# Values cast once for a pair of chunks, weights loaded earlier, and w_out in runs of four rows, in a fused recurrence and squared-ReLU kernel

## The chip, the cores and the metric

The kernel runs on one core of a Trainium2 chip. The metric is the device time of one execution in microseconds (us); lower is better. Each comparison ran the changed kernel and the kernel before on the same chip in the same rounds. Every ratio in this text is the mean time of one kernel's fast runs over that of the other's of the same rounds, with a 95% interval, so it is not quite the ratio of the medians that stand beside it. "Faster" and "slower" as verdicts mean by more than 2%.

Engines: PE is TensorE's matmuls, PEld its weight loads, DVE is VectorE, ACT ScalarE, POOL GpSimd, SP SyncE.

## The reference

A gated linear recurrence over 768 steps for 4 x 8 heads of width 48, then a two-layer FFN with the square of a ReLU:

```
f = 1 / (1 + exp(-f_logit))
state = f[t] * state + outer(k[t], v[t]);  y[t] = q[t] @ state      # 768 steps, 32 heads
x = y as (3072, 384);  h = max(x @ w_in, 0);  out = (h * h) @ w_out # w_in (384, 2048), w_out (2048, 384)
```

Inputs and output are fp32; the matmuls run in bf16.

## The kernel before

The recurrence is computed in 24 chunks of 128 steps, taken in 12 pairs ("attention"). Two chunks make one FFN group of 256 columns: `mm1` multiplies by w_in into `hp` (576 matmuls), ACT or DVE apply ReLU and square, `mm2` multiplies by w_out into `op` (384 matmuls). A small planner inside the kernel simulates all steps with estimated durations and fixes the order of each engine's instructions when the kernel is built. On the chip each engine then keeps to that order. The names in the lines below: `pc` are the running sums of log f of a pair, `tr` transposes of q and k, `at` the products of k and q within a chunk, `am` these times a mask, `ds` a pair's contribution to the state, `sz` the state, `yp` a chunk's y, `xp` and `xT` its transpose; `vx` and `vz` are the values in bf16, in `vz` some of them moved to the other 64 partitions; `idle` is filler that no result needs. `LEAD` shifts the rank of attention against the FFN in the plan. The planner also has a model of the DMA queues: each transfer has an estimated time (`data=`), and GpSimd's queue gets 0.7 of the engines when both queues are busy.

The parts that matter here (cuts marked `...`):

```python
    LEAD = 8
    PACE = [7, 10, 14, 16, 16, 18, 18, 18]        # after which input each weight slice is issued
    ...
    w_in = const.tile([C, KS, d_ff], BF16)         # one tile, 128 x (3 x 2048)
    w_out = const.tile([C, FS, d_model], BF16)
    wo_view = moe_w_out.rearrange("(fs p) f -> p fs f", p=C)
    ...
            if kind == "i":
                nc.gpsimd.dma_start(w_in[:, :, s * FW:(s + 1) * FW], wi_view[:, :, s * FW:(s + 1) * FW])
            else:
                nc.gpsimd.dma_start(w_out[:, s * FQ:(s + 1) * FQ, :], wo_view[:, s * FQ:(s + 1) * FQ, :])
        ...
        plan.add(f"cw{kind}{s}", "POOL", 0.8, fn, after=after, rank=-1, data=(2.8, 0))
    ...
        def vx():                                  # the half that has to change partitions
            st["vx", n] = work.tile([C, H, D], BF16, tag="vx", bufs=3, name="vx")
            for z, j, vt in halves(n):
                nc.gpsimd.tensor_copy(st["vx", n][z], vt[z, 1 - j])
        ...
        def vs():                                  # DMA moves it: vz <- vx
            ...
        def vc():                                  # the half that stays
            for z, j, vt in halves(n):
                nc.gpsimd.tensor_copy(new_vz()[z, j], vt[z, j])
    ...
                        nc.tensor.matmul(ds[j][:, pr, :], a[z, NP + pr, r],
                                         (vt[z, j] if r == j else vo[z])[:, 2 * pr:2 * pr + 2, :].rearrange("p h d -> p (h d)"), ...)
    ...
                        nc.tensor.matmul(hp[:, x, :], w_in[:, ks, (f + x) * C:(f + x + 1) * C], xT[:, ks, lo:lo + W], ...)
```

## Time and profile before

| kernel before | |
|---|---|
| time, median of 3 | 193.49 us (192.4 to 193.5) |
| span of the profiled run | 190.7 us |
| PE / PEld / DVE / ACT / POOL busy | 92 / 70 / 65 / 66 / 49% |
| first hp matmul, first op matmul | 24.0 us, 51.6 us |
| slices of w_in issued | 13.6, 22.2, 32.9, 40.5 us |
| slices of w_out issued | 41.2 to 43.9 us |

The share of TensorE is an average over two regimes. Up to some 60 us the core loads inputs at a full DMA and TensorE often has nothing useful to do; from there to 181 us it is full. So a change earns time only by getting useful matmuls done early. The prediction below shows the lines.

### The profile page before, as it was taken

To read this page: it belongs to the slowest core of one execution; us is meant where nothing else is said; L and a number is where in the kernel's file an instruction comes from. 1 tells how busy PE (TensorE), PEld (TensorE's weight loads), DVE (VectorE), ACT (ScalarE), POOL (GpSimd) and SP (SyncE) were. 2 spreads that over 40 slices of the span, in tenths; PEclk is the share of its full clock that TensorE was granted. 3 is DMA by queue.
4 is the path that set the end of the run, shared out by engine and by line. 5 is a ranking of instruction groups with operands and counts; after the bars stand their busy time and mean duration, and the time that the engine had idled before them with its cause. 6 is when DMAs were issued, how large, how long until landed. Compare 5 with 4: busy or idle time off the path is not lost.

```text
span 190.7 us, 4962 instructions
## 1 busy us (share of the span) xinstructions
PE 176.0 (92%) x1953; PEld 132.8 (70%) x1953; DVE 124.9 (65%) x240; ACT 125.5 (66%) x239; POOL 93.2 (49%) x194
## 2 busy tenths in 40 slices
PE   7578789898999999999999999999999999999991
PEld 7466577786787766667677777677786777777760
DVE  7568897989978847726977646975666735433200
ACT  3646578879879887143896577588485765755521
POOL 7588539595902393926973484652663224000000
PEclk9969999999999999999999999999999999999998
DMA  6999999999998079999999989999561374121122
GB/s 156 261 263 238 270 211 272 243 273 207 204 207 206 3 135 295 209 284 207 218 279 132 262 159 293 186 244 231 98 138 21 65 136 80 22 62 46 41 56 68
DMA packets 77719, 33.29 MB, mean 175 GB/s; under 512 B 71808, under 2 KB 76736, under 8 KB 77696
## 3 DMA queue, kind: packets, MB, share of 16 engines
q1 hardware_dynamic: 71488, 25.11, 65.9%
q0 software_dynamic: 6208, 7.87, 20.2%
q8 instruction: 15, 0.25, 0.6%
q14 instruction: 8, 0.07, 0.1%
HBM read 25.17 MB, written 4.72 MB: 157 GB/s over the span
## 4 chain that ended last, share of the span: by engine, by line
PE 72%; DVE 10%; ACT 6%; POOL 5%; DMA 3%; issue 2%; POOLq 0%; ACTq 0%
PE op L640 32%; PE hp L595 27%; DVE az L423 4%; DMA w_in<-in_moe_w_in_dram 3%; PE at L515 3%; PE yp L541 3%; PE pc L389 2%; ACT ep L412 2%; POOL mask L326 2%; PE ds L479 2%; DVE am L525 1%; DVE le L400 1%; ACT en L412 1%; POOL sz L502 1%; PE pc L392 1%
## 5 line engine op out<-in xcount | busy, mean ns | idle before, releaser
L595 PE MATMUL hp<-xT,w_in 128*128 128x256 bf16 x576 | 75.3, 273 | 4.1 <-ACT hr L602 1.6
L640 PE MATMUL op<-w_out,hT 128*128 128x384 bf16 x384 | 72.9, 326 | 0.0
L595 PEld LDWEIGHTS <-w_in 128*128 128x128 bf16 x576 | 54.6, 98 | 17.1 <-issue 4.5
L602 ACT ACTIVATE hr<-hp 128x512 bf16<-128x512 f32 x82 | 48.4, 596 | 24.7 <-PE hp L595 23.2
L611 DVE TENSOR_TENSOR hT<-hr 128x512 bf16<-128x512 bf16 x69 | 30.3, 443 | 33.8 <-ACT hr L602 33.3
L640 PEld LDWEIGHTS <-hT 128*128 128x128 bf16 x384 | 35.9, 98 | 18.5
L502 POOL TENSOR_TENSOR sz<-tm,en 48x192 bf16<-48x192 f32 x40 | 21.6, 540 | 32.2 <-DVE tm L493 18.8
L525 DVE TENSOR_TENSOR am<-at,mask 128x512 bf16<-128x512 f32 x48 | 31.5, 681 | 4.3 <-PE at L515 4.3
L656 POOL DMA_DIRECT2D out_dram<-ob x36 | 19.2, 537 | 29.0 <-ACT ob L650 29.0
L650 ACT COPY ob<-op 128x384 f32<-128x384 f32 x22 | 10.5, 476 | 16.6 <-PE op L640 16.0
L609 ACT ACTIVATE hT<-hr 128x512 bf16<-128x512 bf16 x27 | 16.9, 631 | 1.0 <-DVE hr L604 0.3
L363 POOL CAST vx<-io_v 64x384 bf16<-64x384 f32 x24 | 13.9, 578 | 4.0 <-DMA io_v<-in_v_dram 2.8
L423 DVE TENSOR_TENSOR az<-io_q,en 128x384 bf16<-128x384 f32 x24 | 14.8, 619 | 0.4 <-ACT en L412 0.3
L423 DVE TENSOR_TENSOR az<-io_k,ep 128x384 bf16<-128x384 f32 x24 | 14.3, 594 | 0.8 <-ACT ep L412 0.8
L381 POOL CAST vz<-io_v 64x384 bf16<-64x384 f32 x24 | 13.6, 569 | 1.1
L674 PE MATMUL idle<-zero 128*128 128x128 bf16 x139 | 12.2, 252 | 1.0 <-DVE zero L312 1.0
L375 POOL DMA_DIRECT2D vz<-vx x24 | 13.1, 549 | 0.0
L350 ACT ACTIVATE e<-io_f 128x768 f32<-128x768 f32 x12 | 10.2, 848 | 3.6 <-DMA io_f<-in_f_logit_dram 3.5
L549 ACT CAST ys<-yp 128x384 bf16<-128x384 f32 x18 | 8.5, 482 | 5.0 <-PE yp L541 5.0
L352 ACT ACTIVATE pz<-e 128x384 bf16<-128x384 f32 x24 | 11.2, 515 | 0.4
L674 PEld LDWEIGHTS <-zero 128*128 128x128 bf16 x139 | 10.6, 117 | 1.0 <-DVE zero L312 1.0
L400 DVE TENSOR_TENSOR le<-pc,pz 128x384 f32<-128x384 f32 x12 | 6.7, 555 | 6.6 <-ACT ep L412 6.1
(54 smaller groups left out, 173.4 us busy)
## 6 DMA issues: line engine op xcount, KB each, us to landing
io_f<-in_f_logit_dram SPq DMA_DIRECT2D x12, 384.0 KB, 5.7
io_k<-in_k_dram SPq DMA_DIRECT2D x12, 384.0 KB, 6.5
io_q<-in_q_dram SPq DMA_DIRECT2D x12, 384.0 KB, 6.4
io_v<-in_v_dram SPq DMA_DIRECT2D x12, 384.0 KB, 6.2
out_dram<-ob POOLq DMA_DIRECT2D x36, 96.0 KB, 3.9
w_in<-in_moe_w_in_dram POOLq DMA_DIRECT2D x4, 384.0 KB, 7.4
w_out<-in_moe_w_out_dram POOLq DMA_DIRECT2D x4, 384.0 KB, 12.6
vz<-vx POOLq DMA_DIRECT2D x24, 48.0 KB, 4.7
```

The source lines that it names most:

```text
L363: nc.gpsimd.tensor_copy(st["vx", n][z], vt[z, 1 - j])
L381: nc.gpsimd.tensor_copy(new_vz()[z, j], vt[z, j])
L423: nc.vector.tensor_mul(z.rearrange("p y (x d) -> p y x d", x=2)[:, :, :, :D], st[x, n].rearrange("p (y x) r d -> p y x r d", x=2)[:, :, :, ...
L502: nc.gpsimd.tensor_mul(nx[r, :, D * x:D * (x + 1)], tm[r, :, D * x:D * (x + 1)], g.unsqueeze(2).to_broadcast([D, NP, D]))
L525: nc.vector.tensor_mul(t, st["at", i][x], mask.rearrange("p y s t -> p y (s t)"))
L595: nc.tensor.matmul(hp[:, x, :], w_in[:, ks, (f + x) * C:(f + x + 1) * C], xT[:, ks, lo:lo + W], start=(ks == 0), stop=(ks == KS - 1), skip ...
L602: nc.scalar.activation(hr[:, :m, :], st["hp", c0, f][:, :m, :], AFT.Relu)
L609: nc.scalar.activation(st["hT", g][:, f:f + m, lo:lo + W], hr[:, :m, :], AFT.Square)
L611: nc.vector.tensor_mul(st["hT", g][:, f:f + m, lo:lo + W], hr[:, :m, :], hr[:, :m, :])
L640: nc.tensor.matmul(st["o", i], hT[:, fs, tt * C:(tt + 1) * C], w_out[:, fs, :], start=(fs == 0), stop=(fs == FS - 1))
L656: (nc.gpsimd if soft else nc.sync).dma_start(out[row + r:row + C:2, :], st["ob", i][P2 * r:P2 * (r + 1)])
L674: nc.tensor.matmul(idle, zero, zero)
```

## The change

Its intent: cast the values of both chunks once (12 larger casts on GpSimd or ACT instead of 48 small ones on GpSimd), move one half by DMA and copy the other on any free engine; issue the weights earlier (PACE, LEAD); read w_out so that each partition gets four consecutive rows in one run of 6 KB. The last needs the hidden units in a matching order, so the weight loads of w_in now take every fourth column.

```diff
-    LEAD = 8
-    PACE = [7, 10, 14, 16, 16, 18, 18, 18]
+    LEAD = 6
+    PACE = [7, 7, 7, 8, 8, 13, 14, 14]
...
-    wo_view = moe_w_out.rearrange("(fs p) f -> p fs f", p=C)
+    wo_view = moe_w_out.rearrange("(s p x) f -> p s x f", p=C, x=FQ)
...
-        plan.add(f"cw{kind}{s}", "POOL", 0.8, fn, after=after, rank=-1, data=(2.8, 0))
+        plan.add(f"cw{kind}{s}", "POOL", 0.8, fn, after=after, rank=-1, data=(2.6 if kind == "i" else 2.3, 0))
...
+        def vx(e):
+            t = st["vx", n] = work.tile([C, 2, H, D], BF16, tag="vx", bufs=3, name="vx")
+            copy[e](t, st["v", n].rearrange("p h r d -> p r h d"))
+        plan.add(f"vx.{n}", "POOL", 1.1, lambda: vx("POOL"), also=[("ACT", 0.75, lambda: vx("ACT"))], ...)
...
+        def vc(e):
+            for j in range(2):
+                z = slice(P2 * j, P2 * (j + 1))
+                copy[e](new_vz()[z, j], st["vx", n][z, j])
...
-                                         (vt[z, j] if r == j else vo[z])[:, 2 * pr:2 * pr + 2, :]...
+                                         vt[z, r, 2 * pr:2 * pr + 2, :]...            # vt is vx now, ds needs no vz
...
-                        nc.tensor.matmul(hp[:, x, :], w_in[:, ks, (f + x) * C:(f + x + 1) * C], xT[:, ks, lo:lo + W],
+                        nc.tensor.matmul(hp[:, x, :], units(ks, f + x), xT[:, ks, lo:lo + W],
...
+    def units(ks, f):
+        s, x = divmod(f, FQ)
+        return w_in[:, ks, s * FW:(s + 1) * FW].rearrange("k (p x) -> k x p", x=FQ)[:, x]
```

More of the change, by code (lines that the diff above doesn't have):

```diff
@@ L261 @@
     st = {}
-    copy = {"ACT": nc.scalar.copy, "DVE": nc.vector.tensor_copy}
+    copy = {"ACT": nc.scalar.copy, "DVE": nc.vector.tensor_copy, "POOL": nc.gpsimd.tensor_copy}
     def both(name, dve, act, fn, **kw):
@@ L299, in fn @@
             else:
-                nc.gpsimd.dma_start(w_out[:, s * FQ:(s + 1) * FQ, :], wo_view[:, s * FQ:(s + 1) * FQ, :])
+                nc.gpsimd.dma_start(w_out[:, s * FQ:(s + 1) * FQ, :], wo_view[:, s])
         after = [] if not pace else [f"vx.{c}"] if x == "v" else [f"{x}{c}"]
-        plan.add(f"cw{kind}{s}", "POOL", 0.8, fn, after=after, rank=-1, data=(2.8, 0))
+        plan.add(f"cw{kind}{s}", "POOL", 0.8, fn, after=after, rank=-1, data=(2.6 if kind == "i" else 2.3, 0))
     touch = const.tile([C, 1], F32)
@@ L353, in attention @@
         plan.add(f"a1.{n}", "ACT", 1.7, a1, after=[f"f{n}"], take=["pz"], give=[f"io_f:f{n}"])
-        def halves(n):
-            vt = st["v", n].rearrange("p h r d -> p r h d")
-            return [(slice(0, P2), 0, vt), (slice(P2, C), 1, vt)]
-        def vx():
-            st["vx", n] = work.tile([C, H, D], BF16, tag="vx", bufs=3, name="vx")
-            for z, j, vt in halves(n):
-                nc.gpsimd.tensor_copy(st["vx", n][z], vt[z, 1 - j])
-        plan.add(f"vx.{n}", "POOL", 0.95, vx, after=[f"v{n}"], take=["vx"], rank=-2)
+        def vx(e):
+            t = st["vx", n] = work.tile([C, 2, H, D], BF16, tag="vx", bufs=3, name="vx")
+            copy[e](t, st["v", n].rearrange("p h r d -> p r h d"))
+        plan.add(f"vx.{n}", "POOL", 1.1, lambda: vx("POOL"), also=[("ACT", 0.75, lambda: vx("ACT"))], after=[f"v{n}"], take=["vx"], give=[f"io_v:v{n}"], rank=-2)
         def new_vz():
@@ L374, in vs @@
                 a_, b_ = slice(P2 * j, P2 * (j + 1)), slice(P2 * (1 - j), P2 * (2 - j))
-                nc.gpsimd.dma_start(t[b_, j].rearrange("p h d -> p (h d)"), st["vx", n][a_].rearrange("p h d -> p (h d)"))
-        plan.add(f"vs0.{n}", "POOL", 0.01, lambda: None, after=[f"vx.{n}"], take=["vz"], rank=-2)
-        plan.add(f"vs.{n}", "POOL", 1.2, vs, after=[f"vs0.{n}"], data=(0.33, 0), rank=-2)
-        def vc():
-            for z, j, vt in halves(n):
-                nc.gpsimd.tensor_copy(new_vz()[z, j], vt[z, j])
-        plan.add(f"vc.{n}", "POOL", 0.95, vc, after=[f"vs0.{n}"], give=[f"io_v:v{n}"], rank=-2)
+                nc.gpsimd.dma_start(t[b_, j].rearrange("p h d -> p (h d)"), st["vx", n][a_, 1 - j].rearrange("p h d -> p (h d)"))
+        plan.add(f"vs.{n}", "POOL", 1.2, vs, after=[f"vx.{n}"], take=["vz"], data=(0.33, 0), rank=-2)
+        def vc(e):
+            for j in range(2):
+                z = slice(P2 * j, P2 * (j + 1))
+                copy[e](new_vz()[z, j], st["vx", n][z, j])
+        plan.add(f"vc.{n}", "DVE", 0.4, lambda: vc("DVE"), also=[("ACT", 0.74, lambda: vc("ACT")), ("POOL", 0.85, lambda: vc("POOL"))], after=[f"vs.{n}"], land=0.2)
         def p1():
@@ L472, in p5 @@
         def p5():
-            vt, vo = st["vz", n], st["vx", n]
+            vt = st["vx", n]
             ds = [psum.tile([C, NP, 2 * D], F32, tag="m%d" % j, name="ds") for j in range(1 if last else 2)]
@@ L479, in p5 @@
                         nc.tensor.matmul(ds[j][:, pr, :], a[z, NP + pr, r],
-                                         (vt[z, j] if r == j else vo[z])[:, 2 * pr:2 * pr + 2, :].rearrange("p h d -> p (h d)"),
+                                         vt[z, r, 2 * pr:2 * pr + 2, :].rearrange("p h d -> p (h d)"),
                                          start=(r == 0), stop=(r == 1), skip_group_check=True)
@@ L519, in p3 @@
             st["am", i] = [None, None]
-        plan.add(f"p3.{i}", "PE", 0.74 if state else 0.42, p3, after=([f"v2{j}.{n}"] if n >= XBAR else [f"v20.{n}", f"v21.{n}"]) + ([f"vx.{n}", f"vc.{n}"] + ([f"p4.{i - 1}"] if i else []) if state else []),
-                 take=["at0", "at1"] + (["m0"] if state and i % NC == NC - 2 else ["m0", "m1"] if state else []), give=[f"vx:vx.{n}"] if state else [], rank=rank)
+        plan.add(f"p3.{i}", "PE", 0.74 if state else 0.42, p3, after=([f"v2{j}.{n}"] if n >= XBAR else [f"v20.{n}", f"v21.{n}"]) + ([f"vx.{n}"] + ([f"p4.{i - 1}"] if i else []) if state else []),
+                 take=["at0", "at1"] + (["m0"] if state and i % NC == NC - 2 else ["m0", "m1"] if state else []), rank=rank)
         def v3(x):
@@ L544, in chunk @@
                  + ([f"p4.{i - 1}"] if j else []),
-                 take=[f"m{j}"], give=[f"am:v3a.{i}"] + ([f"ts:v20.{n}" if n >= XBAR else f"ts:v21.{n}", f"vz:vs0.{n}", f"az:v1k1.{n}", f"en:a2n1.{n}"] if j else []), rank=rank)
+                 take=[f"m{j}"], give=[f"am:v3a.{i}"] + ([f"ts:v20.{n}" if n >= XBAR else f"ts:v21.{n}", f"vz:vs.{n}", f"vx:vx.{n}", f"az:v1k1.{n}", f"en:a2n1.{n}"] if j else []), rank=rank)
         def a3(e):
```

## The prediction

> **What bounds the kernel now.** I read the page first, then stretches of time, then the chain of waits, then GpSimd's timeline. In the page, the busy shares of the engines and the slices:
>
> ```profile
> PE 176.0 (92%) x1953; PEld 132.8 (70%) x1953; DVE 124.9 (65%) x240; ACT 125.5 (66%) x239; POOL 93.2 (49%) x194
> ...
> PE   7578789898999999999999999999999999999991
> ...
> DMA  6999999999998079999999989999561374121122
> ```
>
> TensorE looks full, but its busy time is modelled and its early share contains 139 matmuls on a tile of zeros (12.2 us), filler that no result needs. So I count useful work by the spacing of starts. In the chain, six matmuls into hp take 0.66 us (0.109 us each) and three into op 0.49 us (0.163 us each). 576 x 0.109 = 62.8 us, 384 x 0.163 = 62.5 us. A pair of chunks of attention takes, from the same chain, 0.51 (pc) + 0.66 (at, twice 0.33) + 0.34 (ds) + 0.74 (yp, twice 0.37) = 2.25 us, and the first five pairs 0.90 (tr) + 0.34 (xp) more, 3.49 us: 5 x 3.49 + 7 x 2.25 = 33.2 us. Together 158.5 us. The last op matmul ends at 186.5 us, so TensorE did no useful work for 28 us. Where? By stretch (the columns are the stretch, its length, then PE, PEld, DVE, ACT and POOL busy, granted clock, DMA share, GB/s):
>
> ```profile
> 0.00:24.00 24.00, 17.42 (x246) 14.53 (x247) 17.60 (x31) 13.10 (x24) 17.00 (x52) 0.93 1.14 238
> 24.00:40.00 16.00, 14.12 (x219) 11.84 (x219) 13.77 (x27) 13.68 (x27) 10.14 (x19) 1.00 1.19 250
> 40.00:60.00 20.00, 19.03 (x242) 15.60 (x240) 18.03 (x36) 17.09 (x34) 10.68 (x20) 1.00 1.23 224
> ```
>
> Up to 60 us the trace has 162 hp and 9 op matmuls and some 4.7 pairs: 17.7 + 1.5 + 16.4 = 35.6 us of work. So 24.4 us of the 28 are lost before 60 us: some 19.5 before the first hp matmul at 24.0 us (attention has done pair 0 and the pc and part of the tr of pair 1 by then, about 4.5 us), some 5 from 24 to 60. After 60 us only 3.6 us are lost: TensorE is the bound there. Up to 60 us DMA is full at 224 to 250 GB/s, and from 40 to 60 DVE (18.0 of 20 us) and ACT (17.1) are nearly full too.
>
> The chain shows what holds the early part:
>
> ```profile
> 27.00 0.51 POOL sz L502
> 27.57 0.51 POOL sz L502
> 28.14 0.50 POOL vx L363
> 28.70 0.51 POOL vx L363
> 29.20 0.52 POOL vz L375
> ...
> 30.31 0.50 POOL vz L381
> 30.87 0.51 POOL vz L381
> 31.46 0.50 POOL sz L502
> 32.02 0.69 POOL sz L502
> ...
> 32.89 6.49 DMA w_in<-in_moe_w_in_dram
> 39.42 1.48 PE hp L595 x12
> ```
>
> The third slice of w_in is issued only at 32.9 us, because GpSimd serves its queue in order and the casts, the two small DMA issues and the state products stand before it. The fourth goes out at 40.5, the four of w_out from 41.2 to 43.9; the first op matmul starts at 51.6 us. For almost all of the first 50 us TensorE thus has only hp work, each two units of which also cost a relu and a square on ACT and DVE.
>
> **What the Trainium skill says.** "DMA: Bandwidth & Descriptors", section "Issuing engines are not separate DMA queues": what GpSimd and SyncE issue interleaves on the same 16 engines. The trace agrees: the weights' DMAs land 7.4 us (w_in) and 12.6 us (w_out) after issue while the input queue is full. So weights moved forward push inputs back. "Perfetto Trace Analysis", "DMA Optimizations": transfers under 2 KB carry much overhead. A slice of w_out is now 512 rows of 1536 B; in runs of four rows it is 128 runs of 6 KB. The page's 71808 of 77719 packets under 512 B are nearly all the inputs', which stay. "SBUF — State Buffer", "Door 1: The DMA port swizzle": two hits in a 16-byte line suffice for full rate. The new w_in reads step 8 bytes (every fourth bf16), so two per line: I expect LDWEIGHTS to stay as it is. No strided weight load is in this trace to confirm it. "VectorE: DVE Perf Modes", "The perf-mode tier table": a bf16 copy in SBUF has a mode 4 times the plain rate. Nothing in the trace is quite that copy either; the nearest, xT from PSUM, took 0.35 us for 128x384.
>
> **The change part by part.**
>
> 1. *Casts.* Removed from GpSimd: 24 casts vx (mean 578 ns) and 24 casts vz (569 ns), 27.5 us in all. Added: 12 casts of 128x768. From 0.51 us (the median) for 384 elements a partition I estimate 0.9 to 1.0 us on GpSimd, 0.8 on ACT (exp of 128x768: 0.85), 12 us on one or the other; and 24 copies of 64x384 bf16 to bf16, which may go to DVE, ACT or GpSimd (the plan in the diff reckons 0.4, 0.74 and 0.85 us for two). So GpSimd loses 15 to 25 us and DVE and ACT gain 5 us if all copies go to DVE (12 x 0.4) and up to 15 if ACT takes the casts too. GpSimd is 49% busy: the sum itself buys nothing, only what stands before something urgent.
>
> 2. *No wait of ds for vz.* p5 now reads both halves of the one cast tile and needs neither the DMA nor the second cast. In the trace chunk 1's at runs at 12.4 us and chunk 0's at with ds only at 15.4, since the second cast of pair 0 ended at 12.9. Chunk 0 is the head of the state chain. It could go first, up to 3 us earlier; but the mask products, pc and az of pair 1 sit on the same DVE, so I take half: the first hp matmul at some 22.5 instead of 24.0 us. Gain 1.5 us.
>
> 3. *Weights earlier (PACE).* Slices 0, 1, 2 of w_in are tied to the third input of pair 1 (13.5 us in the trace), slice 3 and the first of w_out to its v (about 16), the rest of w_out to f and k of pair 3. With the plan's 2.6 us of DMA time a slice and its assumed 0.7 of the engines for GpSimd's queue, a slice takes 3.7 us; four from 13.6 us on make 28.5. So w_in is in by some 27 to 30 us instead of about 48 (40.5 plus the 7.4 to landing), w_out by 45 to 50 instead of about 57 (43.9 plus 12.6). The two groups of the first four chunks give 2 x (48 x 0.109 + 32 x 0.163) = 20.9 us of TensorE work, of which the op half (10.4 us) needs no relu or square. That is more than the 5 us lost between 24 and 60.
>
> 4. *What it costs.* Five slices are 12.5 us of DMA time; pair 2's inputs come up to 10 us later, and its chunks at some 40 to 44 us. The 20.9 us above nearly fill that hole. DVE and ACT, nearly full, are given the new copies: a relu and square a unit pair of 0.60 + 0.43 us against 0.65 us of TensorE. So of the 5 us I count 3 recovered.
>
> 5. *w_out in runs of four rows.* Saves perhaps 0.5 us of DMA time a slice (2 us in all), hidden. *LEAD 6*: attention gets a lower rank against the FFN; with work to choose from it only reorders. I count zero.
>
> Sum: 1.5 + 3 = 4.5 us, less 0.3 us for new in-order stalls of DVE and ACT in the full stage: 193.5 - 4.2 = 189.3 us. The tail after the last matmul (186.5 to 190.7 us) is untouched.
>
> **Rivals.** (a) *Inputs starve.* Weights displace the inputs, attention of pairs 2 and 3 slips by 10 us and TensorE idles at 36 to 45 us: the loss moves rather than shrinks, 192 to 194 us. For it: DMA full up to 60 us. Against: it is nearly idle from 60 to 70 us (0.32, 62 GB/s), so inputs have slack later, and the weights' bytes are needed anyway. (b) *DVE and ACT become the early bound.* With weights there, hp runs at the pace of relu and square; at 88% busy in 40 to 60 us only some 10% is left, gain 1 to 2 us, 191.5 to 192.5. Against: op work comes sooner. (c) *Strided weight loads are slower.* PEld's spacing would exceed 0.109 us and each of 576 matmuls pay; 20 ns each would be 11.5 us, time 200. Against: the 16-byte line. (d) *All of it works:* the full 3 us in part 2 and 5 in part 3, 185.5 us.
>
> **Range and chances.** The mechanism of part 3 is visible on the chain, and PACE and LEAD look tuned for the new casts, so slower is unlikely. Two per cent is 3.9 us, just under my 4.2, so the border runs through the middle: faster 0.55, same 0.41, slower 0.04. Range 185.5 (rival d) to 192.3 (rivals a, b).
>
> **What would show each step.** Part 1: GpSimd busy falls to 70 to 80 us and one cast per pair. Part 2: the first ds before 14 us, the first hp at 21 to 23 us. Part 3: w_in slices issued at 13 to 17 us, first op matmul at 35 to 40 instead of 51.6, w_in no longer on the chain between 30 and 40 us, and over 185 hp and 30 op matmuls before 60 us. Part 4: io landings longer than 6 us early on. After 60 us the matmul spacings 0.109 and 0.163 us must be as before; a hp spacing above that, or fewer matmuls by 60 us, makes the prediction wrong.

## The result

The changed kernel is slower: 199.84 us median (198.69 to 200.11, 4 runs) against 193.2 us (192.4 to 193.5, 4 runs), ratio 1.0339 (1.0284 to 1.0393).

First the page of the changed kernel, the busy shares and the slices of TensorE and its clock:

```profile
PE 179.3 (91%) x1955; PEld 141.3 (71%) x1955; DVE 131.2 (66%) x265; ACT 133.9 (68%) x250; POOL 65.4 (33%) x146
...
PE   7875827988998999999999999999999999999990
...
PEclk9997975999999999999999999999999999999999
```

GpSimd lost 28 us of work as intended; DVE gained 6 and ACT 8. The totals say nothing about the loss, but the sixth slice of TensorE (24.7 to 29.7 us) fell to 2 tenths, and the granted clock to 7 tenths in it and 5 in the slice after it. The same three stretches as in the prediction, in the changed kernel (stretch, length, busy time of PE, PEld, DVE, ACT, POOL, then granted clock, DMA share, GB/s):

```profile
0.00:24.00 24.00, 18.04 (x229) 15.19 (x230) 14.83 (x25) 14.03 (x26) 14.67 (x48) 0.93 1.11 224
24.00:40.00 16.00, 10.61 (x141) 8.76 (x142) 9.43 (x20) 7.60 (x15) 2.24 (x4) 0.79 1.15 244
40.00:60.00 20.00, 18.85 (x222) 16.06 (x221) 17.93 (x38) 15.37 (x29) 6.17 (x14) 1.00 1.14 243
```

From 24 to 40 us TensorE did 141 matmuls instead of 219 (26 and 21 of them filler), every engine was idler than before, and the granted clock was 0.79 instead of 1.00. DMA was as full as before. TensorE's timeline there (in brackets: how long it was idle just before, and what ended that), and the lines of the chain of waits in the same stretch, which take the place of GpSimd's queue and the third slice in the chain of the kernel before. First the same hp group in the kernel before, then the changed kernel:

```profile
24.04 1.47 PE L595 MATMUL hp<-xT,w_in 128*128 128x256 bf16 x12 [1.16 <-ACT xT L564]
```

```profile
26.43 0.27 PE L590 MATMUL hp<-xT,w_in 128*128 128x256 bf16 x1 [0.25 <-ACT xT L559]
31.04 2.51 PE L590 MATMUL hp<-xT,w_in 128*128 128x256 bf16 x11 [4.35 <-DMA w_in<-in_moe_w_in_dram]
```

```profile
10.63 6.10 DMA vz<-vx
16.73 0.14 issue
16.86 0.49 PE yp L536 x8
...
20.09 10.82 DMA w_in<-in_moe_w_in_dram
30.91 0.14 issue
31.04 2.51 PE hp L590 x11
```

One hp matmul ran at 26.4 us. The second waited 4.35 us for a DMA of w_in, the one issued at 20.1 us. That is the fourth slice (counted from 1 here; the expectations count from 0); slice 1 went out at 15.1, slices 2 and 3 at 16.1 and 17.0. The first twelve hp matmuls need only the first slice. When the wait ended, 11 matmuls took 2.51 us, which is 0.23 us each, twice the usual 0.109: from 27 to 34 us the granted clock was 0.51 to 0.52.

Why does it wait for a slice that it does not read? The built program names the waits of each instruction. Its first weight loads of w_in, with the DMA semaphores that they wait for (slices 1 to 4 signal on DMASW2, 3, 4 and 7):

```
changed kernel:  507 Ldweights w_in [waits DMASW2]          509 Ldweights w_in [waits DMASW7,DMASW4,DMASW3]
the same with contiguous loads (a_contig below):
                 507 Ldweights w_in [waits DMASW2]   579 [waits DMASW3]   633 [waits DMASW4]   761 [waits DMASW7]
```

With contiguous loads each slice is waited for where it is first read. With stepped loads the second load of the program waits for all of them. w_in lies in SBUF as three blocks of 2048 columns, one for each 128 rows, and a slice is 512 columns of each block. The framework that places the waits must take the stepped read of block 1 and the block-wise writes of slices 2 to 4 to overlap. That it compares the ranges from first to last byte would fit the stepped reads: the first load, of block 0, was not made to wait for the others, and the range of every slice's write covers block 1. But the contiguous load of block 1 lies in these ranges too and was not made to wait, so for contiguous reads the comparison must be finer. This reading of the mechanism is inferred; that the waits are there is read from the program.

### The profile page after: what moved, and what is told of

Its sections match the earlier page's. It is cut to its first block, busy times and chain, and to the rows that moved or that the text cites. A ratio compares the mean times of both kernels' runs of the same rounds, so it can differ in the third digit from the quotient of the medians.

```text
span 197.8 us, 4968 instructions
## 1 busy us (share of the span) xinstructions
PE 179.3 (91%) x1955; PEld 141.3 (71%) x1955; DVE 131.2 (66%) x265; ACT 133.9 (68%) x250; POOL 65.4 (33%) x146
## 3 DMA queue, kind: packets, MB, share of 16 engines
q0 software_dynamic: 4672, 7.87, 19.8%
## 4 chain that ended last, share of the span: by engine, by line
PE 63%; DMA 14%; ACT 9%; DVE 5%; issue 3%; POOL 3%; POOLq 0%; ACTq 0%; DVEq 0%
PE op L641 27%; PE hp L590 25%; DMA vz<-vx 9%; DMA w_in<-in_moe_w_in_dram 5%; PE yp L536 3%; PE at L510 3%; ACT hr L597 2%; POOL mask L326 2%; ACT vx L357 2%; PE pc L384 2%; ACT ep L407 1%; PE ds L474 1%; DVE am L520 1%; ACT hT L604 1%; ACT en L407 1%
## 5 line engine op out<-in xcount | busy, mean ns | idle before, releaser
L590 PE MATMUL hp<-xT,w_in 128*128 128x256 bf16 x576 | 78.6, 276 | 4.6 <-DMA w_in<-in_moe_w_in_dram 4.3
L641 PE MATMUL op<-w_out,hT 128*128 128x384 bf16 x384 | 76.4, 326 | 0.0
L590 PEld LDWEIGHTS <-w_in 128*128 128x128 bf16 x576 | 62.4, 115 | 13.8 <-issue 5.1
L597 ACT ACTIVATE hr<-hp 128x512 bf16<-128x512 f32 x77 | 45.5, 595 | 37.9 <-PE hp L590 36.8
L606 DVE TENSOR_TENSOR hT<-hr 128x512 bf16<-128x512 bf16 x60 | 25.7, 432 | 34.9 <-ACT hr L597 34.4
L604 ACT ACTIVATE hT<-hr 128x512 bf16<-128x512 bf16 x36 | 22.6, 632 | 1.2 <-DVE hr L599 0.2
L418 DVE TENSOR_TENSOR az<-io_q,en 128x384 bf16<-128x384 f32 x24 | 13.6, 566 | 1.0 <-ACT en L407 0.9
L599 DVE TENSOR_SCALAR hr<-hp 128x512 bf16<-128x512 f32 x19 | 13.0, 686 | 1.4 <-PE hp L590 1.1
L536 PE MATMUL yp<-vz,am 128*128 128x48 bf16 x192 | 9.2, 185 | 4.4 <-DMA vz<-vx 4.0
L536 PEld LDWEIGHTS <-am 128*128 128x128 bf16 x192 | 7.4, 97 | 5.2 <-issue 3.3
```

The lines of the kernel that those rows point to most:

```text
L418: nc.vector.tensor_mul(z.rearrange("p y (x d) -> p y x d", x=2)[:, :, :, :D], st[x, n].rearrange("p (y x) r d -> p y x r d", x=2)[:, :, :, ...
L536: nc.tensor.matmul(o_, w, r, start=(y == 0), stop=(y == len(ops) - 1), skip_group_check=True)
L590: nc.tensor.matmul(hp[:, x, :], units(ks, f + x), xT[:, ks, lo:lo + W], start=(ks == 0), stop=(ks == KS - 1), skip_group_check=True)
L597: nc.scalar.activation(hr[:, :m, :], st["hp", c0, f][:, :m, :], AFT.Relu)
L604: nc.scalar.activation(st["hT", g][:, f:f + m, lo:lo + W], hr[:, :m, :], AFT.Square)
L606: nc.vector.tensor_mul(st["hT", g][:, f:f + m, lo:lo + W], hr[:, :m, :], hr[:, :m, :])
```

## The experiments

Theory 1: this false wait is the loss. Rivals: the early weights starve attention of its inputs (theory 2), or the stepped weight loads are slow in themselves (theory 3). All results were correct except the three where a wrong result is announced. The rounds ran on several chips, so each run is compared with the kernel before of its own rounds, and runs of different rounds by these ratios.

### a_tiles: four tiles for w_in

```diff
-    w_in = const.tile([C, KS, d_ff], BF16)
+    w_in = [const.tile([C, KS, FW], BF16, name=f"w_in{s}") for s in range(NW)]
-        return w_in[:, ks, s * FW:(s + 1) * FW].rearrange("k (p x) -> k x p", x=FQ)[:, x]
+        return w_in[s][:, ks].rearrange("k (p x) -> k x p", x=FQ)[:, x]
```

> Edit: the changed kernel with w_in held as four tiles, one for each slice, read with the same step of 8 bytes. In the changed kernel the second weight load of the first hp group waits for slices 1, 2 and 3 of w_in, of which it reads nothing; with four tiles the built program has one wait per slice, at the first load that reads it. Theory 1 (this false wait is the loss): the stall of 4.35 us at 26.7 us and the slow clock after it (11 hp matmuls in 2.5 us instead of 1.2) go, 5 to 7 us faster than the changed kernel: 193 to 195 us. Theory 2 (the early weights displace the inputs, attention starves): at most 2 us faster, 198 us. Theory 3 (the stepped weight loads, 113 instead of 98 ns, are the loss): no gain, since the step stays.

Measured: 193.59 us (before 192.8), ratio 1.0008 (0.9935 to 1.0081). TensorE's timeline of this run:

```profile
26.94 1.47 PE L590 MATMUL hp<-xT,w_in 128*128 128x256 bf16 x12 [0.25 <-ACT xT L559]
```

All twelve matmuls of the first four units of 128 columns, which is the whole first slice, run at once at full clock. Nothing else was changed (in the built programs every engine has the same instructions in the same order), and 3.3% (6.4 us) is gone. The stall of 4.35 us and some 1.3 us of slow clock (2.51 - 11 x 0.109) make 5.7 us of it visible. Theory 1 holds; theories 2 and 3 cannot be the difference to the changed kernel.

### a_contig: old layout of w_out, contiguous loads

```diff
-        return w_in[:, ks, s * FW:(s + 1) * FW].rearrange("k (p x) -> k x p", x=FQ)[:, x]
+        return w_in[:, ks, f * C:(f + 1) * C]          # and wo_view as in the kernel before
```

> Edit: the changed kernel with the old layout of w_out (one row a partition, 1536 B) and contiguous weight loads from the one tile of w_in; the order of all instructions is that of the changed kernel. Theory 1 (false wait): as a_tiles within 1 us, 193 to 195 us, since the built program again waits slice by slice. Theory 3 (step in the weight loads costs): faster than a_tiles by over 2 us, hp loads back at 98 ns. Theory 2: at most 2 us faster than the changed kernel. If the runs of four rows are worth anything in DMA time, a_contig is up to 1 us slower than a_tiles.

Measured: 194.33 us, ratio 1.0082 (1.0038 to 1.0126). The other way to remove the false wait also removes the loss, except for 0.8%. It is not faster than a_tiles, so theory 3 has no support. The weight loads' records (count, then min/median/max in ns) of the changed kernel, and of a_contig:

```profile
L590 PEld LDWEIGHTS <-w_in x576: 110/113/152, 26.0 to 187.0; 128*128 128x128 bf16 x192
```

```profile
L590 PEld LDWEIGHTS <-w_in x576: 95/98/100, 25.8 to 182.5; 128*128 128x128 bf16 x192
```

The step makes each record 15 ns longer. In the full stage six hp matmuls still take 0.66 us in the chain of the changed kernel, as before: the longer load does not lengthen the spacing of 0.109 us.

### b_runs and b_runs_tiles: only the runs of four rows

The kernel before with wo_view and the stepped `units` of the change, first with one tile, then with four tiles as above.

> Edit: the kernel before with only the runs of four rows and the stepped reads of w_in, one tile. Its built program makes the second weight load wait for slice 1 too (issued at 22.2 us before, landed about 29.5), and makes the later slices' DMAs wait for reads that came before them in the program. Theory 1: first hp group stalls from 24 to some 29 us, 2 to 6 us slower than before: 195.5 to 199. Theories 2 and 3: 2 has nothing to say here (before's PACE): 193; 3: some slowdown with hp spacing above 0.109 us all through.

Measured: b_runs 214.47 us, ratio 1.1132 (1.1067 to 1.1197). The mechanism was as expected, the size was not. TensorE's hp matmuls around each new slice in its timeline:

```profile
24.01 0.27 PE L595 MATMUL hp<-xT,w_in 128*128 128x256 bf16 x1 [1.16 <-ACT xT L564]
29.48 2.54 PE L595 MATMUL hp<-xT,w_in 128*128 128x256 bf16 x11 [5.20 <-DMA w_in<-in_moe_w_in_dram]
...
38.92 0.27 PE L595 MATMUL hp<-xT,w_in 128*128 128x256 bf16 x1
46.85 1.26 PE L595 MATMUL hp<-xT,w_in 128*128 128x256 bf16 x5 [7.67 <-DMA w_in<-in_moe_w_in_dram]
...
61.17 1.26 PE L595 MATMUL hp<-xT,w_in 128*128 128x256 bf16 x5 [5.32 <-DMA w_in<-in_moe_w_in_dram]
```

I had counted one stall. With the old PACE the three later slices are issued far apart (22.2, 39.7 and 56.0 us), so each gives a stall of its own: 5.20 + 7.67 + 5.32 = 18.2 of the 21.7 us. The pattern is always the same: one matmul runs (the last of these is hidden in a group of seven before 56 us), its successor waits for a slice that it does not need. In the built program the third and fourth slice's DMAs also wait for TensorE, the false conflict in the other direction.

> Edit: b_runs (214.5 us: before with only the runs of four rows and stepped loads) with w_in as four tiles. Theory 1 (all of b_runs' loss is the false wait): within 0.7% of before, 192 to 194.5 us, no wait of TensorE for w_in over 1 us. Rival (stepped loads cost of themselves): 194.5 us or more, with hp spacing above 0.109 us in the full stage.

Measured: 192.87 us, ratio 0.9996 (0.9953 to 1.0039), five rounds. With four tiles the whole 11% is gone, while loads still step (113 ns). The one expected detail that missed: TensorE waited 1.4 us once for w_in, not under 1. So in this order of instructions the runs of four rows and the stepped loads cost and gain nothing measurable. Two other pairs differ by the same edit, with opposite signs: a_tiles is 0.7% below a_contig, a_tiles_oldpace (below) 0.8% above c_casts. I take these for scatter between different programs; no run shows where it comes from.

### b_pace: only PACE and LEAD

```diff
-    LEAD = 8
-    PACE = [7, 10, 14, 16, 16, 18, 18, 18]
+    LEAD = 6
+    PACE = [7, 7, 7, 8, 8, 13, 14, 14]
```

> Edit: the kernel before with only PACE and LEAD of the changed one. Theory 1: no false wait here, so the early weights give what I predicted for them, 1 to 3 us faster than before: 190 to 192.5. Theory 2 (attention starves behind the weights): slower than before by 3 us or more, 196 or above.

Measured: 193.55 us, ratio 1.0043 (1.0012 to 1.0074). Neither theory: no gain and no loss. The first op matmul came at 39.4 us instead of 51.6, as predicted. But up to 60 us the trace counts 126 hp and 37 op matmuls against 162 and 9 before: 126 x 0.109 + 37 x 0.163 = 19.8 us of FFN work against 19.1, and the same 88 yp matmuls of attention. Op work took the place of hp work, little was added. In built programs with this PACE, LEAD 6 and 8 give TensorE the same order up to the 288th hp matmul (some 109 us in the trace of b_pace) and another after it. So LEAD has no part in the early stage; alone it was not run.

### c_casts and a_tiles_oldpace: the casts without the new PACE

c_casts is a_contig with the old PACE and LEAD, so only the casts are left; a_tiles_oldpace is a_tiles with the old PACE and LEAD.

> Edit: only the casts of the change (one cast of a whole pair on GpSimd or ACT, one half moved by DMA, the other copied); w_out's old layout, contiguous weight loads, old PACE and LEAD. Theory A (my part 2: chunk 0 goes first because ds no longer waits for vz): first hp at 22 to 23 us, 1 to 2 us faster than before, 191 to 192. Theory B (TensorE in order waits at yp for the DMA of vz, as in the changed kernel from 14 to 16.9 us, and chunk 1 comes later): first hp no earlier than 24 us, time 192.5 to 194.5.

Measured: 193.32 us, ratio 1.001 (0.996 to 1.0061). Theory B. TensorE's timeline of c_casts:

```profile
12.38 0.40 PE L510 MATMUL at<-ts 64*128 64x128 bf16 x8 [0.34 <-DVE ts L445]
...
16.86 0.41 PE L536 MATMUL yp<-vz,am 128*128 128x48 bf16 x8 [2.68 <-DMA vz<-vx]
17.19 0.60 PE L510 MATMUL at<-ts 64*128 64x128 bf16 x8
17.73 0.82 PE L384 MATMUL pc<-pz,ut 128*128 128x384 bf16 x2
...
26.95 1.47 PE L590 MATMUL hp<-xT,w_in 128*128 128x256 bf16 x12
```

Chunk 0 does go first (at 12.4 us). But the plan put yp next, which needs the DMA of vz, and TensorE stood 2.7 us; chunk 1's at and pair 1's pc came behind it, at 17.2 and 17.7 us instead of 12.4 and 12.9. They could have run from some 14.2 us on, as c_vw40 below does; before that chunk 1's at waits for chunk 0's mask products. The first hp group came 3 us later than before, not 1.5 us earlier. The plan reckons 0.33 us for the move and 1.6 us for its start and receipt; behind the full input queue it takes up to 6.8 us to land in this run.

> Edit: a_tiles (casts, runs of four rows, four tiles of w_in) with the old PACE and LEAD. Against c_casts it differs only in the runs of four rows and the stepped loads. If the larger runs are worth DMA time: up to 1 us faster than c_casts; if the stepped loads (113 ns) cost anything: slower, by 576 times the excess over 0.109 us, at most 2 us. My expectation: within 0.7 us of c_casts.

Measured: 194.82 us, ratio 1.0093 (1.0048 to 1.0137). That is 1.5 us (0.8%) above c_casts where 0.7 was the limit: a miss. The built program has c_casts' order on every engine, so only the runs and the stepped loads differ, and b_runs_tiles above finds no cost for these; the cause stays open.

### l_pace and l_before: light weights

```diff
-                nc.gpsimd.dma_start(w_in[:, :, s * FW:(s + 1) * FW], wi_view[:, :, s * FW:(s + 1) * FW])
+                nc.gpsimd.dma_start(w_in[:, 0, s * FW:(s + 1) * FW], wi_view[:, 0, s * FW:(s + 1) * FW])
...      # w_out: one row block of four; the matmuls read w_in[:, 0, ...] and w_out[:, fs // FQ * FQ, :]
```

> Wrong result on purpose. Edit: b_pace (before with the new PACE and LEAD) where each weight DMA brings only a part (one of three row blocks of w_in, one of four of w_out) and the matmuls read that part for all; the order of the instructions is that of b_pace, and no engine does less. Theory D (in b_pace the gain of early weights is paid back because their bytes push the inputs of pairs 1 to 4 back): 3 us or more faster than b_pace, 188.5 to 190.5, pair 2's inputs land 5 us earlier than in b_pace. Theory E (DVE and ACT are the bound early, or the order on GpSimd): within 1.5 us of b_pace, 192 to 193.5.

> Wrong result on purpose, the control of l_pace. Edit: the kernel before with the same light weight DMAs. Theory D: the bytes of the weights are paid here too, in another place; 1 to 3 us faster than before (190 to 192), less than l_pace against b_pace because the late w_out hides the wait for inputs less. Theory E: within 1 us of before.

Measured: l_pace 192.71 us, ratio 0.9989 (0.9944 to 1.0034); l_before 191.84 us, ratio 0.9938 (0.9894 to 0.9983). Theory D falls in this form: without most of the weights' bytes b_pace's order gains only some 1 us (ratio 0.9989 against 1.0043), not 3. The control l_before gains 1.2 us by its ratio, inside theory D's 1 to 3 us. The stretch from 40 to 60 us, first in b_pace, then in l_pace:

```profile
40.00:60.00 20.00, 18.26 (x227) 14.16 (x225) 17.38 (x35) 15.56 (x32) 9.58 (x18) 1.00 1.22 252
```

```profile
40.00:60.00 20.00, 18.26 (x225) 13.93 (x223) 17.10 (x34) 15.56 (x32) 10.06 (x19) 1.00 0.56 129
```

DMA is half idle in l_pace and TensorE does the same work at the same pace, so in this stretch it is not the DMA that sets it; the order of the instructions is what both share, with DVE busy for some 17 of the 20 us. Counting the built program shows how the plan changed that order:

```
hp matmuls in TensorE's order before the pc of    pair 3    pair 4
kernel before                                       24        72
b_pace                                              72       126
changed kernel                                      78       138
bn12                                                48        72
```

In the traces the first exp of pair 3 starts at 29.7 us before, and at 39.3 and 38.4 us in b_pace and l_pace: late with the light weights too, so by the order.

### bn12, bm12, cn12, cn5: the same early weights, attention kept early

```diff
-    ... rank=-1, data=(2.8, 0))      # bn12 and bm12; in cn12 and cn5 from 2.6 and 2.3
+    ... rank=-1, data=(1.2, 0))      # 0.5 in cn5; bm12 also PACE = [7, 8, 10, 13, 14, 15, 16, 17]; all four have LEAD = 8
```

> Edit: b_pace (before with the new PACE), where only the DMA time that the plan reckons for a slice of weights is cut from 2.8 to 1.2 us; nothing else about the DMAs changes, only the order that the plan makes of the engines' work. In b_pace's order 72 hp matmuls stand before the pc of pair 3 and 126 before that of pair 4; in before 24 and 72; here 48 and 72. (LEAD 8 instead of 6 changes no instruction's place with this PACE.) Theory F (the early weights make the plan believe the inputs late, so it puts attention of pairs 3 and 4 behind FFN work, in the trace 10 and 13 us later than before): at least 1.5 us faster than b_pace, 190 to 192, pair 3's first exp before 36 us instead of 39.3. Theory G (DVE and ACT bound the early stage, whatever the order): as b_pace, 193 to 194.

> Edit: as bn12 with a milder PACE, [7, 8, 10, 13, 14, 15, 16, 17]. Theory F: 190.5 to 192.5, since pairs 3 and 4 stand early (42 and 72 hp before them) and w_out still comes 5 to 10 us before that of the kernel before. Theory G: 193 to 194.

> Edit: a_contig (casts, new PACE, old layout of w_out, contiguous weight loads), where only the DMA time that the plan reckons for a slice of weights is cut to 1.2 us. 48 and 78 hp matmuls before the pc of pairs 3 and 4 instead of 78 and 138. Theory F: 1.5 us or more faster than a_contig (194.3), 191 to 193. Theory G: 193.5 to 195.

> Edit: as cn12 with 0.5 us. 48 and 72 hp before the pc of pairs 3 and 4, but the plan now believes weights almost free and may put matmuls before their weights are in. Theory F: 191 to 193.5, with waits of TensorE on w_in or w_out in the trace. Theory G: 193.5 to 195.

Measured: bn12 204.05 us, ratio 1.0568 (1.051 to 1.0626); bm12 198.28 us, 1.0263 (1.0202 to 1.0323); cn12 201.29 us, 1.041 (1.0346 to 1.0475); cn5 202.18 us, 1.0473 (1.0419 to 1.0528). All four are slower, and theory F falls. (LEAD 8 instead of 6 does change the place of instructions here, contrary to what was expected, but only from some 72 us on or later.) The list of who waited for whom in bn12 (total us, times, longest):

```profile
POOL vx L363 <- DMA io_v<-in_v_dram: 11.1, 3, 8.6
...
ACT e L350 <- DMA io_f<-in_f_logit_dram: 6.6, 3, 3.3
PE op L640 <- DMA w_out<-in_moe_w_out_dram: 6.6, 2, 3.7
```

The plan no longer knew what the weights cost, so it put attention where its inputs had not landed: GpSimd stood 8.6 us at one cast, and everything behind it in the order stood too. So the late attention in b_pace fits the late inputs; the next run tests it.

### l_bn12: bn12's order with light weights

> Wrong result on purpose. Edit: bn12 (204.0 us) with the light weight DMAs of l_pace; TensorE's order is that of bn12, instruction for instruction. Theory D2 (the bytes of early weights push the inputs back; in b_pace the plan had given way by putting attention late, so light weights could not help there): at least 10 us faster than bn12 and faster than l_before (191.8): 186 to 191.5. Theory G (DVE and ACT bound the early stage): no faster than l_before, 192 or above, with DVE and ACT above 90% busy from 24 to 60 us.

Measured: 193.42 us, ratio 1.0029 (0.9985 to 1.0072). In the same order of TensorE's instructions, the bytes of the weights cost 10.6 us (204.05 against 193.42): early weights do push the inputs back. But the second half of the expectation missed: it is no faster than before, nor than l_before. Theory G had its time right; of its busy shares (over 90% from 24 to 60 us) it just falls short: DVE was busy 12.1 and 18.8 us and ACT 13.4 and 17.9 us of the 16 and 20 us to 40 and 60, 86 and 87% over all, but DVE 94% in the second stretch. So theory G is neither shown nor excluded. The two stretches of l_bn12:

```profile
24.00:40.00 16.00, 13.51 (x184) 10.84 (x182) 12.10 (x24) 13.35 (x26) 10.71 (x22) 1.00 1.11 256
40.00:60.00 20.00, 19.57 (x246) 14.81 (x243) 18.78 (x38) 17.89 (x35) 13.07 (x25) 1.00 1.11 262
```

Up to 60 us this run had 120 hp and 44 op matmuls (20.3 us of work), a little more than before; from 60 to 140 us TensorE was then idle for 3.8 us (80 us less 18.6, 18.7, 19.6 and 19.3), against 0.6 us in the kernel before.

### c_vw25, c_vw40 and a_tiles_vw40: the plan is told how long vz takes

```diff
         plan.add(f"vs.{n}", "POOL", 1.2, vs, ...)
+        plan.add(f"vw.{n}", f"vw{n}", 4.0, lambda: None, after=[f"vs.{n}"], land=0)   # 2.5 in c_vw25
-        plan.add(f"p4.{i}", ..., after=[f"v3b.{i}", f"vs.{n}", f"vc.{n}"] ...
+        plan.add(f"p4.{i}", ..., after=[f"v3b.{i}", f"vw.{n}", f"vc.{n}"] ...
```

> Edit: c_casts (193.3 us), where the plan is told that the DMA of vz takes 2.5 us longer to land; this puts pair 0's second at and pair 1's pc before the first yp in TensorE's order, in c_casts they stand behind it and wait with it for the DMA until 16.9 us. Theory H (this wait eats the gain of the casts): pair 1's pc at 13 to 14.5 us instead of 17.7, first hp at 24 us or before instead of 27.0, 1 to 2.5 us faster than c_casts, 191 to 192.5. Theory I (the early order is hidden anyway, the end is set by the inputs' arrival from pair 2 on): first hp earlier but the time as c_casts within 0.7 us.

> Edit: as c_vw25 with 4.0 us. Theory H: as c_vw25 within 1 us; the second yp moves behind pair 1's tr too. Theory I: as c_casts within 0.7 us.

> Edit: a_tiles (the whole change with four tiles of w_in, 193.6 us) with the 4.0 us for vz in the plan. In its order 54 and 114 hp matmuls stand before the pc of pairs 3 and 4 instead of 78 and 138. Theory H: 1 to 3 us faster than a_tiles, 190.5 to 192.5, and then faster than before. Theory I: 193 to 194.5.

> No edit: c_vw40 again. If the gain is real: ratio to before 0.988 to 0.997 again, 191 to 192.5 us. If it was chance: interval about 1.

Measured: c_vw25 193.48 us, ratio 1.002 (0.9978 to 1.0062); c_vw40 191.83 us, 0.9928 (0.9883 to 0.9973), and again with five rounds 191.98 us, 0.9954 (0.9923 to 0.9986); a_tiles_vw40 193.42 us, 1.0035 (0.9959 to 1.011). TensorE's timeline of c_vw40, to be held against that of c_casts:

```profile
14.76 0.39 PE L511 MATMUL at<-ts 64*128 64x128 bf16 x7 [0.37 <-DVE am L521]
...
15.38 0.50 PE L385 MATMUL pc<-pz,ut 128*128 128x384 bf16 x2
...
16.53 0.36 PE L537 MATMUL yp<-vz,am 128*128 128x48 bf16 x8
...
22.95 1.47 PE L591 MATMUL hp<-xT,w_in 128*128 128x256 bf16 x12
```

The work that was ready now stands before yp, which no longer waits for the DMA. The first hp group comes at 22.95 us, 4 us before c_casts and 1.1 us before the kernel before. The kernel gains 0.5 to 0.7% on before: small, found twice, the one version with a right result that beats both kernels. c_vw25 puts pc first too, but later (16.2 us) and its first hp group at 25.0, and gains nothing: it misses theory H on each count. a_tiles_vw40 has its first hp at 23.5 us and is not faster than a_tiles, as theory I said: with the new PACE the early start is lost again further on. The 4.0 us also change the plan's later order (156 hp matmuls before the pc of pair 5 instead of 138 in c_casts), so that the early start alone makes the gain is likely, not shown.

## Why the prediction was wrong

I predicted 189.3 us; it was 199.84. The sum was 1.5 + 3 - 0.3 us of gain.

**The step that failed, above all, is part 3**, "w_in is in by some 27 to 30 us". The slices did land then (the last at 31.0), but the step took for granted that each hp group waits only for its own slice. The stepped reads, which I weighed under rival (c) only as a question of load speed, changed the waits of the built program, so the first group waited for the last slice. That is worth 6.4 us (ratio 1.0339 against 1.0008 with four tiles, 1.0082 with contiguous loads), and alone it turns the result from "same" into "slower". None of my rivals had it. Rival (c) did name the stepped loads but not this way. LDWEIGHTS did not stay as it was, as I had expected (113 ns instead of 98), but this cost nothing: b_runs_tiles 0.9996.

**Part 2** (first hp at 22.5 us, 1.5 us gained): half right. ds went first at 12.6 us, as I said. What I left out is that TensorE keeps its order and yp would stand before other work, waiting for a small DMA behind a full queue (6.1 us). The first hp came at 26.4 us. When the plan knew that, it came at 22.95 us and the gain was 0.5 to 0.7%, about 0.9 to 1.4 us; that this is close to my 1.5 may be luck, since the later order changed too. My reason for chunk 0's late at (the cast that ended at 12.9 us) was incomplete: the mask products of chunk 1, which free its PSUM buffers, ended only at 14.4, and filler stood in the order until 15.4.

**Part 3, the 3 us of early weights:** even without the false wait they gave nothing (b_pace 1.0043). The first op matmul did come at 39.5 us in a_tiles (44.7 in the changed kernel). But the count that I asked for (over 185 hp and 30 op matmuls by 60 us) was 138 and 29 in a_tiles: op work came in place of hp work. I had taken the 20.9 us of work of two groups as an addition; the counts show that hp work fell nearly as much as op work grew. That part 4's price, pairs 3 and 4 ten and thirteen us later in b_pace, is what took it away, is argued, not shown. Nor did w_out come as early as I said: only its first slice did (20.9 us), the other three went out at 45.8 to 47.1 us in the changed kernel and 40.7 to 42.0 in a_tiles, where the kernel before has 42.2 to 43.9. Rival (a), "the loss moves rather than shrinks, 192 to 194 us", had the right number for the change without its false wait. Its mechanism, starving inputs, is shown for bn12's order alone (10.6 us against l_bn12); in b_pace's order the light weights gain 1 us.

**Part 1** was right in kind: 12 casts, all on ACT (824 ns, I reckoned 0.8), GpSimd down to 65 us (70 to 80 predicted), DVE and ACT together up by 15 us, the upper end of my 5 to 15. **Part 5** was right for the runs, which are worth nothing measurable; LEAD was not run alone. After 60 us the spacings were as predicted.

**What stays open:** why early weights buy nothing even when their bytes are taken away (l_bn12 is not faster than l_before). Its early count of work was no worse. DVE was 94% busy from 40 to 60 us there, so the bound may lie with it; and the DMA was still full up to 60 us (share 1.11), light weights or not. The plan's order differs in the later stage too, and I have no run that holds that stage fixed and changes only the early one.

## What to carry to other kernels

When a change alters how a tile is read, look at the waits in the built program, not only at the speed of the read: a strided view of one large tile can be made to wait for every transfer into it, and a tile for each transfer removes that. In a kernel whose order is fixed when it is built, the estimates are part of the kernel: one DMA reckoned at 2 us that takes 6 puts ready work behind a wait. And early transfers are not free when the queue is full; count the useful work by a fixed time, before and after, instead of assuming that it adds.

## What the Trainium skill lacked or had wrong

- No page mentions that waits placed by a framework can cover more than an instruction reads. Here a stepped read of one tile cost 6.4 us in the changed kernel and 21.7 us in b_runs.
- "DMA: Bandwidth & Descriptors", section "Anatomy of one DMA", gives a fixed cost of about 2.0 us plus bytes at 436 GB/s, which makes an estimate of 2.1 us for the 48 KB of one half of vz. Beside a full input queue the runs show 6.1 us for pair 0 in the changed kernel and 1.8 to 9.6 us over all (median 4.0). The time in the queue is missing from that formula.
- "SBUF — State Buffer", section "Door 1: The DMA port swizzle", says that two hits in a 16-byte line keep full rate. For weight loads with a step of 8 bytes, so two elements in a line, the record is 113 instead of 98 ns: the load itself did not keep its rate, though the kernel's time is unchanged (ratio 0.9996).
- "TensorE: Matmul & The Clock Gate", section "Weight-path perf modes — Fast Weight Load (FWL) and DoubleRow", lists "packed or strided" as read patterns of fast weight loads without a figure for the strided one. The same 113 against 98 ns may be one; whether the fast load is on here no run shows.
